# Attention, expert 0 and expert 1's first block ordered by a plan over the graph of steps

## The chip, the cores and the metric

The kernel runs on one core of one Trainium2 chip. The metric is the device time of one execution in microseconds (us). The engines are TensorE (PE: matmuls; PEld: its weight loads), VectorE (DVE), ScalarE (ACT), GpSimd (POOL) and SyncE (SP, which only issues DMAs). Each engine carries out its own instructions in the order in which the program gives them, and semaphores hold an instruction until what it reads or overwrites is ready.

## The reference

```python
def _attn_ref(q, k, v, mem_k, mem_v):        # (4, 8, 768, 64); 8 memory rows a head
    for c in range(768 // 32):               # chunks of 32 queries
        k_full = concat(mem_k, k[16 before .. 8 behind the chunk]); v_full likewise
        scores = q_c @ k_full.T / sqrt(64)
        a = exp(scores - max(scores)); a = a / (sum(a) + 1e-09)
        out[chunk] = a @ v_full

def _moe_ref(x, w_gate, w1, w2):             # x (3072, 512), 8 experts, 1024 hidden
    P = exp(x @ w_gate - max)
    for _ in range(8):
        P /= P.sum(1) + 1e-09; P /= P.sum(0) + 1e-09; P *= N / E
    return sum(P[:, e] * (relu(x @ w1[e]) @ w2[e]) for e in range(8))

def _moe2_ref(x, w_in, w_out):               # 512 -> 2048 -> 512
    h = relu(x @ w_in)
    return (h * h) @ w_out

reference = moe2(moe(attention(q, k, v, mem_k, mem_v)))
```

## The kernel before

Numbers are carried as pairs of 16-bit halves (hi and lo), so a product of two matrices is three matmuls: lo with hi, hi with lo, hi with hi.

Attention goes by 32 tiles of 96 queries (`NA`, `TQ`), each three chunks, against 120 keys and 8 memory rows. One tile is a chain of 22 steps: load q, k, v (`a_load`); the largest magnitude per row and over the tile (`a_scale`, `a_all`, `a_row_max`, `a_spread`, `a_scale2`); split into hi and lo (`a_split`, `a_split_lo`); transpose q and k by a DMA (`a_tqk`); scores with a mask (`a_scores`), their row maximum (`a_max`), its transpose (`a_mt`, `a_mtc`); the scores again, transposed, less the maximum (`a_st`); exponential (`a_exp`) and its split (`a_asplit`, `a_asplit_lo`); times v (`a_av`); normalization (`a_norm`), split (`a_xsplit`, `a_xsplit_lo`) and a DMA transpose into `xt` (`a_tx`), the input of the experts.

Expert 0 goes by 13 blocks of tokens (two of 128, then eleven of 256). A block's first layer is four pairs of 24 matmuls (`l1_pair`), each followed by a relu on ScalarE and its lo half on VectorE (`l1_lo`); the second layer has 24 matmuls for each 128 tokens, in two halves (`l2_half`). `gate` gives the logits of 128 tokens. When all logits are there, `balance_steps` runs the eight rounds of the reference's loop, with one column sum on PE in each. Expert 1's first block (`PLAIN`: 14 products `prod` and 8 second-layer halves) follows expert 0; its results wait in PSUM until the balance is done (`l2_acc`). From expert 1's second block on, loops of products with their own hooks order the rest of the kernel.

PSUM has eight banks. Two (`ps`) serve the experts and the gate; attention has one (`mm`) for the small transposes and maxima, three (`sc`) for scores and two (`av`) for the output. There are three load buffers for q, k and v (`raws`), two of them in memory that results need later, so `raw_of` uses three for 18 tiles and two after that. Where several steps share memory or a bank, the framework puts in the waits.

The order of this first stage is written out by time: every step has an offset within its tile (`STEPS`), every tile a start (`ta`: in the end 10.957 us after the last), the weights of expert 0 and 1, the gate and the balance have times of their own (`W_AT`, `TE`, `SK`), and expert 0's pairs and halves advance a clock of 2.65 us each, stretched by `STR`. The steps are sorted by these times and issued in that order:

```python
def when(i, n):
    r = min(1.0, i / RAMP)
    t = ta(i) + (1 - r) * STEPS[n][1] + r * STEPS[n][0]
...
ev.sort(key=lambda x: x[:2])
for _, _, fn, a in ev:
    fn(*a)
```

Lines of the profile: 265 the tile's maximum, 269 a cast behind it, 288 its spread, 343 and 485 the two DMA transposes, 361 mask and 373 scores, 408 and 411 transposed scores and what is subtracted, 441 to 449 the output, 458 to 461 normalization, 509 gate, 553 column sum, 594 weights of expert 0, 790 to 792 expert 0's first layer, 1285 to 1287 second layers, 929 products of expert 1 and later, 1299 adding expert 1's result.

## Time and profile before

| | us |
|---|---|
| median of three runs | 2578.11 |
| lowest, highest | 2573.98, 2579.66 |
| span of the profiled execution | 2577.2 |
| PE busy in it | 2426.7 (94%) |
| DVE, ACT, POOL busy | 1906.5, 1339.0, 1339.5 |
| start of expert 1's second block | 582.78 |

The profiled execution is one run of the program, and its span reaches from the first to the last instruction. PE's busy time counts overlapping matmuls once and is no measure of how close PE is to its best; the distance from one matmul's start to the next is. The granted clock is the share of PE's full speed (1.00 is 2.4 GHz, the lower level is 1.2 GHz, and a number between is a mean over the stretch). A time in brackets behind a timeline row is how long the engine stood idle before it, and what ended that.

### The profile page before, as it was taken

What the parts mean: (1) busy time and instruction counts of PE and PEld (TensorE: products, weight loads), DVE (VectorE), ACT (ScalarE), POOL (GpSimd) and SP (SyncE); (2) the same over time, 40 slices, a digit from 0 to 9 for tenths busy, and PEclk for the clock granted to TensorE, in tenths of its full rate; (3) what the DMA queues carried; (4) which work ended last, traced back from release to release, by engine and by line L of the source; (5) the groups of instructions that cost most, each with busy time, mean ns of one, the idle gap of its engine ahead of it and who ended that gap; (6) DMA issues with size and microseconds to landing.
All of it is one profiled execution on the core that took longest, in us unless ns stands there. A gap on an engine that the chain in (4) does not pass through costs nothing.

```text
span 2577.2 us, 53497 instructions
## 1 busy us (share of the span) xinstructions
PE 2426.7 (94%) x21970; PEld 2035.4 (79%) x21970; DVE 1906.5 (74%) x2932; ACT 1339.0 (52%) x2323; POOL 1339.5 (52%) x1120
## 2 busy tenths in 40 slices
PE   2789889889999999999999999999999989999999
PEld 1566566556668888888888888888888878888888
DVE  7778677476567888788788878877758887667555
ACT  4444444233344555556555555555556666766454
POOL 2312112352563675567557465746746767866443
PEclk9889899999999999999999999999999999999999
DMA  7688676232335345334444544443333366663221
GB/s 167 96 142 144 105 124 101 72 104 77 126 120 177 132 143 185 129 127 135 170 151 132 168 138 151 148 150 127 113 103 132 117 170 155 169 168 123 77 68 54
DMA packets 377916, 334.31 MB, mean 130 GB/s; under 512 B 256584, under 2 KB 311368, under 8 KB 371016
## 3 DMA queue, kind: packets, MB, share of 16 engines
q1 hardware_dynamic: 294054, 309.99, 41.8%
q10 hardware_dynamic: 83618, 20.91, 4.5%
q8 instruction: 171, 2.80, 0.4%
q14 instruction: 73, 0.60, 0.1%
HBM read 215.50 MB, written 77.07 MB: 114 GB/s over the span
## 4 chain that ended last, share of the span: by engine, by line
PE 79%; DVE 11%; DMA 3%; ACT 3%; issue 2%; POOL 2%; SPq 1%; ACTq 0%; DVEq 0%; POOLq 0%
PE pbA L929 35%; PE pbE L929 18%; PE pbB L929 8%; PE pb L929 4%; PE py L1285 3%; PE py L1286 3%; PE py L1287 3%; PE ph L790 1%; PE ph L792 1%; PE ph L791 1%; DVE amx L265 1%; DVE hp L1127 1%; DVE acc L1240 1%; DMA raw<-in_q_dram 1%; DMA qkT<-qk 1%
## 5 line engine op out<-in xcount | busy, mean ns | idle before, releaser
L929 PEld LDWEIGHTS <-wb 128*128 128x128 f16 x5184 | 508.3, 98 | 71.6 <-issue 10.4
L929 PEld LDWEIGHTS <-hp 128*128 128x128 f16 x4608 | 450.8, 98 | 57.9 <-DVE hp L1127 3.0
L929 PEld LDWEIGHTS <-wx 128*128 128x128 f16 x3888 | 380.8, 98 | 52.7 <-issue 7.6
L929 PEld LDWEIGHTS <-xt 128*128 128x128 f16 x3456 | 338.2, 98 | 48.4 <-DVE xt L1127 7.3
L929 PE MATMUL pbA<-w2p,hp 128*128 128x256 f16 x2304 | 291.4, 273 | 3.7 <-DVE hp L1127 1.9
L929 PE MATMUL pbA<-S,wb 128*128 128x256 f16 x2304 | 283.6, 273 | 6.5 <-ACT S L1057 2.7
L929 PE MATMUL pbE<-xt,wx 128*128 128x256 f16 x2304 | 284.1, 273 | 4.5 <-DVE u L1062 3.7
L1057 ACT ACTIVATE u<-pbA 128x512 f32<-128x512 f32 x180 | 106.5, 592 | 187.0 <-PE pbA L929 185.8
L432 POOL TENSOR_TENSOR aT<-e,aT 128x768 f16<-128x768 f32 x32 | 52.5, 1640 | 243.5 <-ACT aT L426 220.0
L929 PE MATMUL pbA<-w2p,xt 128*128 128x256 f16 x1152 | 157.1, 273 | 0.0
L929 PE MATMUL pbE<-xt,hp 128*128 128x256 f16 x1140 | 156.6, 274 | 0.0
L929 PE MATMUL pbE<-xt,xt 128*128 128x256 f16 x1140 | 156.2, 273 | 0.2 <-POOL xt L1127 0.2
L1285 PE MATMUL py<-w2p,hp 128*128 128x512 f16 x384 | 149.0, 388 | 7.0 <-DVE hp L799 3.7
L1057 ACT ACTIVATE xt<-pbA 128x512 f32<-128x512 f32 x147 | 86.5, 592 | 127.0 <-PE pbA L929 124.9
L1286 PE MATMUL py<-w2p,hp 128*128 128x512 f16 x384 | 149.0, 388 | 0.0
L1287 PE MATMUL py<-w2p,hp 128*128 128x512 f16 x384 | 148.7, 387 | 0.0
L1127 POOL TENSOR_TENSOR hp<-u,hp 128x512 f16<-128x512 f32 x86 | 114.8, 1335 | 64.9 <-ACT hp L1120 64.9
L929 PE MATMUL pbA<-S,wx 128*128 128x256 f16 x1152 | 141.4, 273 | 2.3 <-ACT xt L1057 0.9
L929 PE MATMUL pbB<-xt,wb 128*128 128x256 f16 x1152 | 141.4, 273 | 0.0
L929 PE MATMUL pbA<-xt,wb 128*128 128x256 f16 x1152 | 141.4, 273 | 0.0
L1062 DVE TENSOR_TENSOR u<-pbE,u 128x512 f32<-128x512 f32 x100 | 68.6, 686 | 94.8 <-ACT u L1057 54.9
L1127 POOL TENSOR_TENSOR xt<-u,xt 128x512 f16<-128x512 f32 x72 | 94.8, 1325 | 55.2 <-ACT xt L1120 55.2
(376 smaller groups left out, 5802.6 us busy)
## 6 DMA issues: line engine op xcount, KB each, us to landing
wst<-in_moe_w_dram SPq DMA_DIRECT2D x80, 512.0 KB
xt<-xdr SPq DMA_DIRECT2D x40, 1024.0 KB
S<-sdr SPq DMA_DIRECT2D x126, 256.0 KB
w2d<-wst SPq DMA_DIRECT2D x32, 512.0 KB
w2p<-w2d SPq DMA_DIRECT2D x32, 512.0 KB
wst<-in_moe_w_dram SPq DMA_DIRECT2D x56, 256.0 KB
...
```

Of the source, the lines that this page charges most:

```text
L265: nc.vector.tensor_reduce(mx, raw, AX.X, ALU.max, apply_absolute_value=True)
L432: nc.gpsimd.tensor_tensor(aT[:, 1], st.pop((i, "e")), aT[:, 0], ALU.subtract)
L790: nc.tensor.matmul(p[:, r], lhsT=w[:, 1], rhs=xh, start=first, stop=False)
L791: nc.tensor.matmul(p[:, r], lhsT=w[:, 0], rhs=xl, start=False, stop=False)
L792: nc.tensor.matmul(p[:, r], lhsT=w[:, 0], rhs=xh, start=False, stop=last)
L929: nc.tensor.matmul(p[:, r], lhsT=w[:, ws], rhs=x[:, xs], start=a, stop=z, skip_group_check=onto)
L1057: nc.scalar.activation(t, p, AF.Copy, scale=sc)
L1062: nc.vector.tensor_tensor(t, p, t, ALU.add)
L1127: eng.tensor_tensor(d[:, 1], t, d[:, 0], ALU.subtract)
L1285: nc.tensor.matmul(p, lhsT=h[:, 1], rhs=w[:, 0], start=first, stop=False)
L1286: nc.tensor.matmul(p, lhsT=h[:, 0], rhs=w[:, 1], start=False, stop=False)
L1287: nc.tensor.matmul(p, lhsT=h[:, 0], rhs=w[:, 0], start=False, stop=last)
```

## The change

The written times go. Every step of the stage, from the first load to the adding of expert 1's first block, becomes a task with an engine, a cost, a priority, the tasks that it comes after, and what it holds (PSUM banks, DMA semaphores). When the kernel is built, `Plan.run` takes again and again the task that can start first (among equals, the one of lowest priority number), and the steps are issued in the order of these starts. Attention's priorities are 100 a tile, expert 0's start at 10000.

With it come changes of the steps:

- `a_scores` and `a_st`: heads of 64 rows on either half of the array. hi x lo, lo x hi and hi x hi are three matmuls of 64 rows a head, where before one of 128 rows did two of them. The mask is 3 rows in place of 96, on rows 0 and 64 (`GRP`), and what `a_st` subtracts is 19 rows (`KR`) in place of 112. So q and k are 16 blocks to transpose, not 20, and GpSimd's copy of q's hi half is gone.
- `avb`: the small maxima and transposes and the gate's logits move into the second of the two banks of attention's output; scores get four banks.
- three load buffers for all tiles, two of them in memory of attention's own; tiles 0 and 2 are loaded by SyncE's queue, the others by ScalarE's; memory rows are loaded only when a buffer turns to another batch.
- `a_scale` and its followers read the upper halves of 32-bit numbers in place, which drops four small VectorE instructions a tile.
- the gate's scale goes through a matmul in place of a GpSimd reduction.
- first-layer pairs are cut in four pieces (`l1_mm`), second-layer halves in four (`l2_part`); weight splits, the balance's column sums and the sums for Strassen's products are cut likewise, so that each piece is one task on one engine.
- the mask set-up is rewritten (more small GpSimd instructions, and nine on ScalarE as three tasks).

The core of the diff:

```diff
+COST = {
+    "load": 1.3, "mx": 1.75, "row": 0.12, "row_mx": 0.28, "all": 0.12, "scale": 0.75, "invx": 0.25,
+    "hi": 1.85, "lo": 2.25, "tqk": 3.1, "scores": 0.95, "max": 1.65, "mt": 0.12, "mtc": 0.25,
+    "st": 1.0, "exp": 1.05, "ahi": 0.85, "alo": 1.7, "av": 0.8, "norm": 1.05, "xhi": 0.65,
+    "xlo": 0.7, "tx": 1.25,
 }
-TA = 10.957
...
-SK = [0.01, 2.7, 2.52, 7.55, 7.55, 7.27, 6.55, 7.55, 7.55, 7.89, 7.55, 7.55, 5.95]
-W_AT = [-5.06, 6.92, 9.11, 14.42, 18.96, 23.87, 33.67, 39.86, -3.33, 28.00, 3.81]
+LAND = {"load": 1.8, "tqk": 4.4, "tx": 1.7, "w": 2.5}
+SLACK = 0.6
+MOVE = {"load": 3.6, "tqk": 4.5, "tx": 1.5, "w1": 1.5, "w2": 1.3}
...
-    raws = [
-        ap_.tile([P, 3, H * D], F32, name="raw0"), acc[NB - 1][:, 0:3, :], acc[NB - 2][:, 0:3, :]
-    ]
+    raws = [ap_.tile([P, 3, H * D], F32, name=f"raw{n}") for n in range(2)]
+    raws.append(acc[NB - 1][:, 0:3, :])
...
-        return i % 3 if i < 3 * LATE // 4 else i % 2
-
+        return i % 3
+
+    avb = psa.tile([P, 2, 512], F32, name="avb")
+    mmb = avb[:, 1, 4 * VP:]
...
-        dq = nc.sync if i < 3 else nc.scalar
+        dq = nc.sync if i in (0, 2) else nc.scalar
...
-            dq.dma_start(
-                out=hd(raw[NW:P, t, :]), in_=mem[b].rearrange("h p d -> p h d")
-            )
+            if mem_in.get((raw_of(i), t)) != b:
+                mem_in[raw_of(i), t] = b
+                dq.dma_start(
+                    out=hd(raw[NW:P, t, :]), in_=mem[b].rearrange("h p d -> p h d")
+                )
...
-        eb = ap_.tile([P, 3], I32, tag="aeb0", name="aeb0", bufs=2)
-        e16 = ap_.tile([P, 3], BF16, tag="ae16", name="ae16", bufs=2)
-        nc.vector.tensor_scalar(eb, mx.bitcast(I32), EXP_MASK, None, ALU.bitwise_and)
-        nc.vector.tensor_copy(e16, eb.bitcast(F32))
-        st[i, "e16"] = e16
+        st[i, "amx"] = mx
 
     def a_all(i):
 
-        p = psa.tile([3, P], F32, tag="mm", name="pmax")
-        nc.tensor.matmul(p, lhsT=st.pop((i, "e16")), rhs=ident, start=True, stop=True)
+        p = mmb[0:3, 0:P]
...
-        scs = [psa.tile([TQ, 4, P], F32, tag="sc", name="sc", bufs=3) for u in range(2)]
-        for sc in scs:
+        scs = [psa.tile([TQ, 4, P], F32, tag="sc", name="sc", bufs=4) for u in range(2)]
+        for g, sc in zip(GRP, scs):
             nc.tensor.matmul(
                 sc,
-                lhsT=onehot,
-                rhs=maskr[:, mask_at(i)].unsqueeze(1).to_broadcast([TQ, 4, P]),
+                lhsT=onehot[g:g + NR],
+                rhs=less[g:g + NR, mask_at(i), 0].unsqueeze(1).to_broadcast([NR, 4, P]),
                 start=True,
                 stop=False,
             )
 
-        for s in range(2):
+        for s in range(3):
             for hh in range(4):
                 for u in range(2):
                     q_, k_ = qk_of(qkT, 2 * hh + u)[s]
                     nc.tensor.matmul(
-                        scs[u][:, hh, :], lhsT=q_, rhs=k_, start=False, stop=(s == 1 and hh == 3))
+                        scs[u][:, hh, :], lhsT=q_, rhs=k_, start=False, stop=(s == 2 and hh == 3))
...
-        p = psa.tile([TQ + 2 * H, TQ], F32, tag="mm", name="pmt")
-        nc.tensor.matmul(p, lhsT=m16s[i % 2], rhs=ident16, start=True, stop=True)
+        p = mmb[0:MR, P + 4:P + 4 + TQ]
...
-        for u in range(2):
-            for hh in range(4):
+        for hh in range(4):
+            for u, g in enumerate(GRP):
                 nc.tensor.matmul(
-                    scs[u][:, hh, :], lhsT=less[:, mask_at(i), 4 * u + hh], rhs=mt,
-                    start=False, stop=(hh == 3))
+                    scs[u][:, hh, :], lhsT=less[g:g + KR, mask_at(i), 4 * u + hh],
+                    rhs=mt[g:g + KR], start=False, stop=(hh == 3))
...
-        o = psa.tile([TQ, 2, 512], F32, tag="av", name="av")
+        o = avb[0:TQ]
...
-        lgp = ps.tile([P, 2, E], F32, tag="ps", name="lgp")
+        lgp = mmb[:, 228:228 + 2 * E].rearrange("p (s e) -> p s e", s=2)
...
-        def cols():
+        def cols_mm():
...
+            st["colsum"] = p
+
+        def cols():
+            p = st.pop("colsum")
...
+        return [load, start, rows] + [cols_mm, cols_rows] * (ITERS - 1) + [cols_mm, cols_end]
...
+    def l1_mm(fp, b, c, n, r, kks):
+
+        if r == 0 and kks[0] == 0:
+            st["l1", fp, b, c] = ps.tile([P, 2, n], F32, tag="ps", name="ph2")
+        p = st["l1", fp, b, c]
+        for kk in kks:
+            w = wb[kk % 2][fp % 2][:, :, 2 * (kk // 2) + fp // 2, r * P:(r + 1) * P]
+            xh, xl = xt[b][:, 0, kk, c:c + n], xt[b][:, 1, kk, c:c + n]
+            first, last = kk == 0, kk == KD - 1
+            nc.tensor.matmul(p[:, r], lhsT=w[:, 1], rhs=xh, start=first, stop=False)
+            nc.tensor.matmul(p[:, r], lhsT=w[:, 0], rhs=xl, start=False, stop=False)
+            nc.tensor.matmul(p[:, r], lhsT=w[:, 0], rhs=xh, start=False, stop=last)
+
...
+    def l2_part(e, t, tl, fs, ev):
+
+        if fs[0] == 0:
...
+        for f in fs:
...
+        class Plan:
+            LAG = {"PE": 0.25, "DVE": 0.1, "ACT": 0.1, "POOL": 0.1}
+
+            def __init__(self, rings):
+                self.tasks, self.bufs = [], rings
+                self.start, self.done = {}, {}
+
+            def add(self, eng, cost, pri, fn, *a, after=(), ring=None, land=0.0, lock=False, dma=0.0):
+                self.tasks.append([eng, cost, pri, fn, a, list(after), ring, land, lock, [], dma])
+                n = len(self.tasks) - 1
+                if ring and ring[0] == "lane":
+                    self.tasks[n][9] = [[n]] * ring[1]
+                return n
...
+            def run(self):
+                free, held, shut, moved = {}, {r: [] for r in self.bufs}, 0.0, 0.0
+                todo = {n: len(x[5]) for n, x in enumerate(self.tasks)}
+                users = {}
+                for n, x in enumerate(self.tasks):
+                    for d in x[5]:
+                        users.setdefault(d, []).append(n)
+                ready = {n: 0.0 for n, c in todo.items() if not c}
+                order = []
+                while ready:
+                    best = None
+                    for n, r in ready.items():
+                        eng, cost, pri, _, _, _, ring, _, lock, _, _ = self.tasks[n]
+                        t = max(r, free.get(eng, 0.0))
+                        if ring:
+                            name, m = ring
+                            for k_ in range(m):
+                                back = len(held[name]) + k_ - self.bufs[name]
+                                if back >= 0:
+                                    for f in self.tasks[held[name][back][0]][9][held[name][back][1]]:
+                                        t = max(t, self.seen(f, eng))
+                        if lock:
+                            t = max(t, shut)
+                        if t < 1e8 and (best is None or (t, pri, n) < best[0]):
+                            best = ((t, pri, n), n)
+                    assert best, [self.tasks[n][3:5] for n in ready]
+                    (t, _, _), n = best
+                    eng, cost, _, _, _, _, ring, land, lock, _, dma = self.tasks[n]
+                    self.start[n] = t
+                    self.done[n] = t + cost + land
+                    if dma:
+                        moved = max(moved, t + 0.5) + dma
+                        self.done[n] = max(self.done[n], moved + 1.8)
+                    if eng:
+                        free[eng] = t + cost
+                    if lock:
+                        shut = t + cost
+                    if ring:
+                        held[ring[0]].extend((n, k_) for k_ in range(ring[1]))
+                    order.append(n)
+                    del ready[n]
+                    for u in users.get(n, ()):
+                        todo[u] -= 1
+                        if not todo[u]:
+                            ready[u] = max(self.seen(d, self.tasks[u][0]) for d in self.tasks[u][5])
+                assert len(order) == len(self.tasks)
+                return [(self.start[n],) + tuple(self.tasks[n][3:5]) for n in order]
+
+        plan = Plan({"lane": 8, "lgp": 1, "pmax": 1, "pall": 1, "pmt": 1, "sc": 4, "av": 1, "ps": 2})
...
+        WAR = {
+            "load": [("lo", 3)], "mx": [("row", 2)], "row_mx": [("all", 2)],
+            "scale": [("lo", 2), ("invx", 2), ("exp", 6)], "hi": [("tqk", 2), ("av", NV)],
+            "tqk": [("st", 2)], "max": [("mt", 2)], "mtc": [("st", 2)],
+            "exp": [("alo", 1)], "ahi": [("av", 2)], "norm": [("xlo", 1)], "xhi": [("tx", 1)],
+        }
+        RING = {"row": ("pmax", 1), "all": ("pall", 1), "mt": ("pmt", 1), "scores": ("sc", 2),
+                "st": ("sc", 2), "av": ("av", 1), "tqk": ("lane", 1)}
+        FREE = {"row": ["row_mx"], "all": ["scale"], "mt": ["mtc"], "scores": ["max", "max"],
+                "st": ["exp", "exp"], "av": ["norm"]}
...
+        LS = [add("ACT", 3.2, 5 + 100 * mv, setup_less, mv) for mv in range(3)]
         for i in range(NA):
...
+            for r, (n, fn) in enumerate(FN.items()):
+                pri = 100 * i - r - (300 if n == "load" else 0)
+                cost = COST[n]
+                eng = ENG[n]
+                if n == "load" and i in (0, 2):
+                    eng = "SP"
+                    cost = 2.5
+                ring = RING.get(n)
+                if n == "load":
+                    ring = ("lane", 3 + 2 * (i % TPB in (0, TPB - 1)) + 2 * (i % TPB < 3))
+                if n in ("tx", "invx"):
+                    two = i * TQ % (P if n == "invx" else BLK) // 32 + 3 > (4 if n == "invx" else 16)
+                    cost *= 2 if two else 1
+                    ring = ("lane", 1 + two) if n == "tx" else None
+                after = [T[i, d] for d in RAW.get(n, ())]
+                after += [T[i - m, d] for d, m in WAR.get(n, ()) if i >= m]
+                after += [T[i - 1, n]] if i and n not in MOVE else []
+                after += LS[mask_at(i):mask_at(i) + 1] if n == "scores" else []
+                T[i, n] = add(eng, cost, pri, fn, i, after=after, ring=ring,
+                              land=LAND.get(n, 0.0), dma=MOVE.get(n, 0.0), lock=n in ("lo", "xlo", "alo", "invx"))
...
+        for w in range(2):
+            pri = (150, 350)[w]
+            for n in range(4):
+                m = 4 * w + n
+                W["load", m] = add("SP", (0.9, 0.5)[w], (-150, 60)[w], (w1_load0, w2_load0)[w], n,
+                                   after=[] if w == 0 else [T[1, "tqk"]], land=LAND["w"],
+                                   dma=MOVE["w1"], ring=("lane", 2 - w))
+                W["max", m] = add("DVE", 1.22, pri, w_max0, m, after=[W["load", m]])
...
+            for f in range(NF // 2):
+                w_in_ = [W["lo", n] for n in range(4)]
+                war = [L2[x] for x in L2 if blk > 1 and x[0] == blk - 2]
+                part = None
+                for r in range(2):
+                    for kks in ((0, 1), (2, 3)):
+                        part_ = add("PE", 0.655 * f_, pri + f, l1_mm, f, b, c, n0, r, kks,
+                                    after=[part] if part else x_in + w_in_, ring=None if part else ("ps", 1))
+                        m0, part = (m0 if part else part_), part_
+                m1 = part
+                rl = add("ACT", 0.15 + 0.45 * f_, -4, l1_relu, f, b, c, n0, blk % 2, after=[m1] + war)
+                lo = add("DVE", 0.15 + 0.55 * f_, -4, l1_lo, f, b, c, after=[rl])
+                holds(m0, lo)
...
+        OP = add("SP", 1.5, -9, open_post, after=list(T.values()) + list(G.values()), land=LAND["w"])
...
+        prev, accs = L2[len(blocks) - 1, 1, 1], {}
+        for n, (item, hooks) in enumerate(zip(PLAIN, jobs(1, 0))):
+            u = item[2] if item[1] == "P" else 1
+            need = [x for c_ in WC[2 * u:2 * u + 2] for x in c_]
+            if item[1] == "L2":
+                need = W2C[2 * item[3]:2 * item[3] + 2]
...
         ev.sort(key=lambda x: x[:2])
         for _, _, fn, a in ev:
+            fn(*a)
+        for _, fn, a in plan.run():
             fn(*a)
```

## Rows read from the trace of the kernel before

**Rows 1.** Windows: busy us of PE, PEld, DVE, ACT, POOL; clock, DMA share, GB/s

```profile
0.00:86.00 86.00, 25.37 (x233) 18.89 (x234) 65.97 (x169) 37.51 (x54) 23.00 (x30) 0.90 0.76 151
...
150.00:275.00 125.00, 116.97 (x1275) 85.24 (x1272) 102.42 (x236) 58.73 (x119) 25.92 (x38) 1.00 0.83 134
275.00:325.00 50.00, 39.94 (x374) 27.16 (x374) 32.23 (x82) 17.96 (x36) 7.60 (x11) 0.86 0.66 101
325.00:478.00 153.00, 142.78 (x1551) 104.42 (x1550) 101.67 (x239) 66.03 (x133) 28.73 (x37) 1.00 0.60 98
478.00:582.80 104.80, 85.58 (x517) 52.48 (x515) 71.92 (x132) 35.49 (x51) 51.01 (x44) 0.92 0.33 113
582.80:2577.20 1994.40, 1966.58 (x17462) 1708.85 (x17461) 1485.89 (x1971) 1094.04 (x1872) 1185.33 (x939) 1.00 0.42 133
```

**Rows 2.** Timeline, 0 to 16 us: start, us, engine or queue, line, instruction

```profile
0.72 5.24 SPq L594 DMA_DIRECT2D acc<-in_moe_w_dram  x8
...
15.76 1.75 DVE L265 TENSOR_REDUCE amx<-raw 128x3 f32<-128x1536 f32 x1 [6.65 <-DMA raw<-in_q_dram]
```

**Rows 3.** Timeline of PE: first products of expert 0 and expert 1's block 1

```profile
86.04 0.30 PE L790 MATMUL ph<-xt,wb 128*128 128x128 f16 x1
...
582.78 0.60 PE L929 MATMUL pb<-xt,wb 128*128 128x256 f16 x4 [2.29 <-DVE acc L1299]
```

**Rows 4.** Groups on PE, 150 to 275 us: busy us, mean ns, idle before

```profile
L790 PE MATMUL ph<-xt,wb 128*128 128x256 f16 x120 | 32.8, 273 | 0.3 <-ACT lg L509 0.3
...
L1285 PE MATMUL py<-w2p,hp 128*128 128x512 f16 x56 | 21.3, 380 | 0.0
```

**Rows 5.** Timeline of PE at 480 us, second layer of expert 0

```profile
480.72 0.38 PE L1285 MATMUL py<-w2p,hp 128*128 128x512 f16 x1
...
481.15 0.38 PE L1287 MATMUL py<-w2p,hp 128*128 128x512 f16 x1
```

**Rows 6.** Timeline of PE, 187 to 193 us: transposed scores, then scores

```profile
187.81 0.78 PE L408 MATMUL sct<-qkT 128*128 128x96 f16 x16
188.52 0.51 PE L411 MATMUL sct<-mt,less 112*128 112x96 f16 x8
188.96 0.16 PE L288 MATMUL pall<-ad,ones 128*128 128x3 bf16 x1
...
191.60 0.60 PE L361 MATMUL sc<-less,onehot 96*96 96x512 bf16 x2
192.04 0.61 PE L373 MATMUL sc<-qkT 128*96 128x128 f16 x8
...
192.58 0.42 PE L373 MATMUL sc<-qkT 64*96 64x128 f16 x8
...
192.93 0.28 PE L790 MATMUL ph<-xt,wb 128*128 128x256 f16 x1
```

**Rows 7.** DMA queues, 150 to 275 us: packets, MB, share of engines

```profile
q1 hardware_dynamic: 34816, 10.10, 54.3%
q10 hardware_dynamic: 25948, 6.49, 28.1%
```

**Rows 8.** Groups on VectorE, 150 to 275 us: a small one

```profile
L269 DVE CAST ae<-aeb 128x3 bf16<-128x3 f32 x10 | 1.7, 172 | 0.3
```

**Rows 9.** Timeline of VectorE at 200 us: normalization of one tile

```profile
200.38 0.15 DVE L458 TENSOR_SCALAR rs<-av 96x8 f32<-96x8 f32 x1
...
200.80 0.69 DVE L461 TENSOR_TENSOR acc<-av,rs 96x512 f32<-96x512 f32 x1
```

**Rows 10.** Timeline of SyncE's queue at 477 us: the last tile's transpose

```profile
477.62 1.21 SPq L485 DMA_TRANSPOSE xt<-x  x1
```

**Rows 11.** Timeline of PE, 527 to 578 us: column sums, expert 1's product

```profile
527.95 0.49 PE L553 MATMUL colsum<-pm,ones 128*128 128x192 f32 x2
528.28 0.93 PE L929 MATMUL pb<-xt,wb 128*128 128x256 f16 x7
...
577.41 0.49 PE L553 MATMUL colsum<-pm,ones 128*128 128x192 f32 x2
```

553 lines of the change are left out of this document (267 added, 286 removed).

## The prediction

> **What bounds the kernel now.** I read the page first (its slices show where TensorE, PE, is not full), then the busy time by stage, and inside one steady stretch the groups of instructions, the timeline of one tile's attention and the DMA queues. The plan orders only what runs before expert 1's second block, and that block's first product starts at 582.78 us [rows 3]. What follows, 1994.4 us with PE busy for 1966.6, is the same text in both kernels [rows 1]; I carry it over unchanged. So the question is when that product starts.
>
> In the first 582.8 us PE is bound in part only. From 150 to 275 us it is busy for 117.0 of 125 us at full clock, and from 325 to 478 for 142.8 of 153 [rows 1]: there it is the bound. Elsewhere it is starved: 25 of the first 86 us, and 39.9 of 50, at a granted clock of 0.86, from 275 to 325 [rows 1]. The first product of expert 0 starts at 86.04 us [rows 3]. From 478 on, when the last tile of attention is transposed (issue at 477.62 [rows 10]), PE is busy for 85.6 of 104.8 us at a clock of 0.92 [rows 1], while the balance chain goes on to its last column sum at 577.41 [rows 11].
>
> What PE has to do there, at steady rates: 256-column matmuls follow each other at 0.11 us (four span 0.60 [rows 3], one takes 0.27 [rows 4]), 512-column ones at 0.215 (480.72 to 481.15 for two [rows 5]). Expert 0's first layer is 13 blocks, two of half width, of 4 x 24 matmuls: 1152 full ones, 126.7 us. Its second layer is 24 x 24 x 0.215 = 123.8. Expert 1's first block is 168 x 0.11 + 96 x 0.215 = 39.1. Eight column sums at 0.33 (527.95 to 528.28 [rows 11]) are 2.6. For attention I take what is left of the steady stretch: 3 x 120 x 0.11 + 3 x 56 x 0.215 = 75.7 us are expert 0's [rows 4], so 49.3 of 125 us went to ten tiles (the count of [rows 8]), 4.9 each with gates, changes of shape and short waits; 32 tiles make 157. Sum 449. The stage took 582.8, so 134 us are PE waiting or slowed.
>
> **The change, part by part.** *Rows of 64.* One tile's scores run from 191.60 to 192.93, 1.33 us; the transposed scores from 187.81 to 188.96, 1.15 [rows 6]. Eight 128-row matmuls span 0.61 us, eight 64-row ones only 0.42, so with the last one's 0.22 taken off they follow at 0.056 and 0.03: two of 64 rows on different halves run side by side [rows 6]. After: 24 of 64 rows at 0.03 are 0.72, the two mask matmuls (now 3 rows, one on either half) 0.22 in place of 0.44, a change of shape 0.09 (192.43 to 192.58, less one pitch): 1.03. The transposed scores: 24 at 0.025 (96 columns) and 8 at 0.0275 are 0.82. Saved: 0.63 a tile; I take 0.6, 19 us in all. Bounds: nothing, if matmuls of 3 and 19 rows do not pair or change the shape too often, and 0.75.
>
> The Trainium skill, "TensorEngine Tiling (Array Packing)", section Key Properties, says that a change of tiling mode drains TensorE, and lists tiles of 32 rows as a mode of their own. By that rule 3 and 19 rows would be another mode than 64, two more changes a tile; at 0.09 each that is 6 us and the sum would give 2500 in place of 2494. No trace here has a matmul of so few rows.
>
> *Less work beside PE.* The transpose of q and k has 16 blocks in place of 20, with x's eight 24 in place of 28: queue q1's 54.3% of 125 us for ten tiles is 6.8 a tile [rows 7] and falls to 5.8; the loads (q10, 28.1%, 3.5 a tile) lose most of the memory rows, about 0.1. Together 9.2 a tile. VectorE (DVE) had 102.4 us for ten tiles [rows 1], 10.2 each; four small instructions go (such as the cast at 0.17 [rows 8]), about 0.75: 9.5. GpSimd loses a copy, ScalarE a quarter of its split instructions. The gate's scale leaves GpSimd's reduction for one matmul and some small DVE instructions, once. None of these ends the path while PE is full, so I cost them at nothing; their cover is PE's own 250.5 / 32 + 4.3 = 12.1 us a tile. They matter as the pace that attention can reach when it goes first: 9.5.
>
> *The start.* Before, SyncE's queue issues eight weight loads (0.72 to 5.96) ahead of tile 0's loads, and DVE's first maximum starts at 15.76 [rows 2]. Now tile 0 goes first: about 8 us. Against that, ScalarE's nine mask instructions stand ahead of tile 1's load on its queue and wait for some twenty small GpSimd instructions. Up to the first product DVE was busy for 66 of 86 us [rows 1], which is over six tiles' worth, where two tiles and four weight maxima are needed: the plan takes the earlier tile first. I put the first product at 60, about midway between 35 (two tiles' DVE time after the first load) and the old 86. About three tiles' attention, 13 us of PE, lies in front of it, so 47 us are lost. Second-layer weights are loaded after tile 1, and a 256-token block needs 2.7 tiles: 8 us more for feeding (0 to 25).
>
> *Small pieces, plan, tail.* Attention has priority, and first-layer pairs (2.6 us) are cut in four. Attention can then end near 50 + 31 x 10.2 = 366 us, with expert 0 far from done. From 478 the first product of expert 1 (528.28) is 50 us off and the balance's last sum 99 [rows 11]; from 370 both are over by 470, under PE's leftover work. What is late next is PE itself, so the 19 us of idle PE there go, and the starved stretch at 275 goes as well, since tiles now have three load buffers throughout. Four score banks end a wait that I count within the 4.9.
>
> *One shared bank.* The added wait: maxima, their spread, the row-maximum transpose, the gate and half of attention's output now lie in one PSUM bank. If the program guards the bank as a whole, each of these five matmul groups waits for the reader of the one before, and behind it on PE's queue stand expert 0's pieces. The readers hold it about 2.1 us of a 10-us tile (the normalization 1.1, from 200.38 to the end of the row at 200.80 [rows 9]; I take 0.25 for each of the others), so a fifth of 4.75 writes meets one, for some 0.45 us: 14 us over 32 tiles. Bounds: 0 and, with every second write held for a whole split (1.8 us), 3.6 a tile.
>
> **Sum.** 250.5 + 39.1 + 2.6 + 32 x 4.3 = 429.8; start 47, feeding 8, bank 14: block 1 starts at 498.8 in place of 582.8, 84 us earlier. The profiled execution's 2577.2 becomes 2493.2; the median of the runs is 0.9 above it: 2494.
>
> **Rivals.** With a fixed order the end is also first tile + 31 x pace + what the plan left for after attention. At a planned 9.5 us a tile PE gets 5.2 us of expert 0 beside each, 161 in all, and 89 + 41.7 = 131 stay behind. So 50 + 31p + 131: a pace of 10.25 gives my 499.
>
> (a) *Transfers set the pace.* DMA was 83% busy in the steady stretch [rows 1], and its need of 9.2 us a tile is nearly the planned pace; a transpose landing late holds the scores, and everything queued behind them on PE. At 11.5: 537.5, 2533 us. Against: the bytes fall, and before, the queues held 12.5 us a tile with PE full. 0.17.
>
> (b) *The shared bank, slower than before.* From a pace of 13 on, 2.7 us a tile over mine, the end is past 582.8. That takes two waits a tile of 1.4 us on readers queued behind DVE's longer instructions, with DVE 82% busy [rows 1] and to be fuller. At a pace of 14: 615, 2610 us. The Trainium skill, "PSUM — Partial Sum Buffer", section PSUM bank collisions raise a hardware error, speaks for it: no two engines may touch one bank on the same partitions at once, so waits have to guard the bank and not the address. No run here shows such sharing. Against: most readers take under 0.3 us. 0.13.
>
> (c) *The start does not move*: weights, mask set-up and first tiles still meet at 86. 429.8 + 86 - 18 + 22 = 520, 2515 us. 0.13.
>
> (d) *PE full from 50 on*, no bank or feeding loss, and attention at 4.0: 420 + 37 = 457, 2452 us. 0.12.
>
> **How the numbers follow.** My case, 2465 to 2530: 0.40. No difference (a measurement of this kernel tells 0.2% at best, 5 us; that is (a) at a pace near 13): 0.05. Faster: 0.40 + 0.17 + 0.13 + 0.12 = 0.82; slower 0.13. A range of 2450 to 2575 leaves out (b) and a little more.
>
> **What would show it.** Right: expert 0's first product near 60; the eight-and-eight patterns of scores at 1.0 us and transposed scores at 0.8; no dip at 275 to 325; attention's last transpose near 370 while expert 0 goes on past 450; a product of expert 1's second block near 500; the same 1994 us after it. Wrong: gaps on PE ahead of attention's output or the maxima, released by DVE's normalization (b); gaps ahead of scores released by the transpose (a); a first product at 80 or later (c); another length of the later part.

## The result, and the profile after

The changed kernel takes 2531.24 us (median; 2530.39 to 2532.41) where the kernel before takes 2577.52: a ratio of 0.9818, 95% interval 0.9804 to 0.9832. That is 46 us less; the forecast was 84 less (2494), inside the range but short by nearly half. The first question is in which stage the difference lies. Busy time by stage of the changed kernel's profiled execution (span 2529.5; columns as in [rows 1]: the stretch, its length, busy time of PE, PEld, DVE, ACT and POOL with counts, granted clock, DMA share, GB/s; the DMA share adds up the times of the packets that start in the stretch, so that a short one can come out above 1):

```profile
0.00:87.50 87.50, 26.89 (x353) 20.27 (x354) 66.88 (x139) 46.96 (x60) 31.46 (x51) 1.00 0.77 147
87.50:150.00 62.50, 50.08 (x685) 38.29 (x686) 41.94 (x87) 26.83 (x55) 8.21 (x14) 0.92 0.85 128
98.00:105.00 7.00, 0.57 (x11) 0.47 (x9) 1.32 (x2) 0.00 (x0) 0.14 (x1) 0.92 1.33 145
150.00:275.00 125.00, 117.67 (x1535) 81.62 (x1535) 104.38 (x223) 62.90 (x117) 25.90 (x33) 1.00 0.94 140
275.00:325.00 50.00, 49.54 (x617) 34.91 (x617) 35.29 (x76) 24.11 (x48) 9.11 (x11) 1.00 0.81 126
325.00:422.00 97.00, 94.48 (x1191) 66.52 (x1184) 60.02 (x129) 44.12 (x87) 15.62 (x17) 1.00 0.51 78
422.00:535.30 113.30, 101.97 (x656) 64.95 (x654) 75.14 (x135) 38.70 (x57) 50.27 (x44) 0.94 0.31 104
535.30:2529.50 1994.20, 1966.54 (x17463) 1708.99 (x17461) 1487.46 (x1971) 1093.96 (x1872) 1186.72 (x939) 1.00 0.42 133
```

The last row is the part after expert 1's second block has begun: 1994.2 us, 1994.4 before. The whole gain is the 47.5 us by which that block starts earlier, and the dip at 275 to 325 of [rows 1] is gone. 28.0 of them are time in which TensorE was idle (122.7 us before the second block, now 94.7). Where the stage begins and ends, on TensorE's timeline (start, duration, line, output and inputs; in brackets the wait before it) and, last, on SyncE's for the end of attention:

```profile
87.38 0.31 PE L361 MATMUL avb<-ident,m 96*83 96x96 f16 x1 [4.67 <-DVE m L355]
87.48 0.31 PE L784 MATMUL ph<-xt,wb 128*128 128x128 f16 x1
...
535.26 0.93 PE L930 MATMUL pb<-xt,wb 128*128 128x256 f16 x7
...
421.77 1.21 SPq L455 DMA_TRANSPOSE xt<-x  x1
```

Expert 0's first product is at 87.48: it has not moved (86.04 in [rows 3]; forecast 60). The second block starts at 535.26 instead of 582.78. Attention's last transpose is issued at 421.77 instead of 477.62 [rows 10]. The forecast had both earlier, near 499 and 366.

One tile's matmuls in the steady stretch, to set beside [rows 6] (scores, then transposed scores):

```profile
196.60 0.41 PE L329 MATMUL sc<-less,onehot 3*96 3x512 bf16 x2
196.95 0.87 PE L341 MATMUL sc<-qkT 64*96 64x128 f16 x24
197.75 0.39 PE L1291 MATMUL py<-w2p,hp 128*128 128x512 f16 x1
...
202.00 0.68 PE L378 MATMUL sct<-qkT 64*128 64x96 f16 x24
202.62 0.34 PE L381 MATMUL sct<-mt,less 19*128 19x96 f16 x8
```

From the first start to the last end, scores take 1.22 us and transposed scores 0.96; in [rows 6] the same is 1.40 and 1.22. From the first start to the start of the next instruction, which is how the prediction read [rows 6], scores take 1.15 instead of 1.33 (196.60 to 197.75) and transposed scores mostly 0.89 instead of 1.15 in those rows (mostly 1.07 in that trace).

### The profile page after: what moved, and what is told of

It reads as the page before. It is cut to its first block, busy times and chain, and to the rows that moved or that the text cites. A ratio compares the mean times of both kernels' runs of the same rounds, so it can differ in the third digit from the quotient of the medians.

```text
span 2529.5 us, 54257 instructions
## 1 busy us (share of the span) xinstructions
PE 2407.2 (95%) x22483; PEld 2015.5 (80%) x22483; DVE 1871.1 (74%) x2759; ACT 1337.6 (53%) x2294; POOL 1327.3 (52%) x1108
## 4 chain that ended last, share of the span: by engine, by line
PE 82%; DVE 12%; ACT 2%; DMA 2%; issue 1%; POOL 1%; ACTq 0%; SPq 0%; DVEq 0%; POOLq 0%
PE pbA L930 36%; PE pbE L930 18%; PE pbB L930 8%; PE pb L930 4%; PE py L1291 3%; PE py L1292 3%; PE py L1293 3%; PE ph L784 1%; PE ph L786 1%; PE ph L785 1%; DVE hp L1128 1%; DVE acc L1241 1%; PE sc L341 1%; DVE smx L350 1%; PE sct L378 1%
## 5 line engine op out<-in xcount | busy, mean ns | idle before, releaser
L1291 PE MATMUL py<-w2p,hp 128*128 128x512 f16 x384 | 147.6, 384 | 7.6 <-DVE hp L921 6.0
L1292 PE MATMUL py<-w2p,hp 128*128 128x512 f16 x384 | 147.1, 383 | 0.0
L1293 PE MATMUL py<-w2p,hp 128*128 128x512 f16 x384 | 146.9, 383 | 0.0
```

Source lines behind the costliest of these rows:

```text
L1291: nc.tensor.matmul(p, lhsT=h[:, 1], rhs=w[:, 0], start=first, stop=False)
L1292: nc.tensor.matmul(p, lhsT=h[:, 0], rhs=w[:, 1], start=False, stop=False)
L1293: nc.tensor.matmul(p, lhsT=h[:, 0], rhs=w[:, 0], start=False, stop=last)
```

## The experiments

All are edits of the changed kernel. Their times stand in one table, with the points of the trace that turned out to matter: expert 0's first product, the issue of the transpose of tile 6 (counted from 0, as everywhere here) and of the last tile, and the first product of expert 1's second block, in us.

| kernel | median | ratio to before, 95% | first product | tile 6 | last tile | second block |
|---|---|---|---|---|---|---|
| the changed kernel | 2531.2 | 0.9804 to 0.9832 | 87.5 | 145.2 | 421.8 | 535.3 |
| mask | 2529.8 | 0.9800 to 0.9838 | 85.4 | 139.9 | 420.3 | 534.8 |
| xbuf | 2550.2 | 0.9874 to 0.9915 | 80.2 | 144.0 | 438.1 | 555.2 |
| sc3 | 2549.8 | 0.9864 to 0.9909 | 87.1 | 145.8 | 431.7 | 555.9 |
| bank | 2533.2 | 0.9812 to 0.9849 | 86.9 | 139.2 | 413.6 | 537.0 |
| bank2 | 2533.5 | 0.9807 to 0.9839 | 87.5 | 142.6 | 422.0 | 536.8 |
| w2dve | 2529.4 | 0.9786 to 0.9823 | 87.2 | 142.7 | 419.8 | 530.4 |
| pieces | 2542.7 | 0.9843 to 0.9874 | 88.1 | 143.3 | 431.4 | 546.4 |
| recost | 2538.0 | 0.9824 to 0.9860 | 80.3 | 141.3 | 415.9 | 540.0 |
| spload | 2519.0 | 0.9751 to 0.9784 | 83.7 | 136.4 | 410.0 | 524.0 |
| nolo | 2529.1 | 0.9788 to 0.9818 | 82.7 | 139.0 | 416.7 | 530.4 |
| now2 | 2533.8 | 0.9806 to 0.9836 | 87.9 | 145.7 | 423.8 | 539.9 |
| three | 2514.2 | 0.9739 to 0.9766 | 83.6 | 134.1 | 407.4 | 518.1 |

The kernel before was run again beside each group of these kernels, and its median lay between 2577.5 and 2580.2: differences of under 3 us between two rows of the table are not told apart.

Read the last two columns first: the second block starts 111 to 124 us after the last tile, whatever was edited. Now read the column of the first product against the median: it says nothing. The two earliest, 80.2 and 80.3, belong to kernels slower than the changed one.

### The start: mask set-up, or the order of the queues?

In the trace of the changed kernel ScalarE's queue begins with the nine mask instructions. They wait for GpSimd, tile 1's load goes out only between them (12.38 to 15.16), and tile 0's split (line 300) comes after them all, though VectorE has its scale ready at 11.5:

```profile
6.52 1.05 ACT L1462 ACTIVATE less<-heads 83x1024 bf16<-83x1024 bf16 x1 [2.38 <-POOL heads L1432]
9.13 2.13 ACT L1465 ACTIVATE less<-maskr 3x1024 bf16<-3x1024 bf16 x2 [1.55 <-POOL maskr L1459]
...
12.38 0.63 ACTq L217 DMA_DIRECT2D raw<-in_k_dram  x1
...
18.77 1.33 ACT L300 ACTIVATE qk<-raw,asc 128x512 f16<-128x512 f32 x2
```

**mask** moves them and nothing else:

```diff
+        order = plan.run()
+        masks = [x for x in order if x[1] is setup_less]
+        order = [x for x in order if x[1] is not setup_less]
+        for x, i in zip(masks, (0, 1, 2)):
+            order.insert(1 + [y[1:] for y in order].index((a_split, (i,))), x)
```

> The changed kernel with its order kept, except that the nine mask instructions (three calls of setup_less) go to ScalarE's queue behind the splits of tiles 0, 1 and 2, instead of ahead of tile 1's load. Theory M (the mask set-up at the head of ScalarE's queue is why the start did not move): tile 0's split, at 18.8 us in the changed kernel, comes at about 12, tile 1's maximum several us before its 19.4, the first product of expert 0 at about 80 instead of 87.5, and the median falls from 2531 to about 2524. Theory Q (what holds the first product is the order of the queues behind it: tile 1's output is normalized at 60.7 but its split waits until 73.6 and its transpose until 81.2 behind work of later tiles): the first tiles come earlier, the first product stays within 2 us of 87.5, and the median within 3 us of 2531.

Tile 1's load went out at 0.79 and tile 0's split ran at 15.32 (not 12: VectorE's first maximum now starts at 11.29 instead of 7.63, behind tile 0's load, which shares the transfers with tile 1's). The first product came at 85.4, not at 80, and the time is the same within the measurement. Theory M falls.

Further down the queue the order is the obstacle. Tile 1's output is normalized from 60.66 on (the row of line 428 on VectorE's timeline). On ScalarE's timeline its split (line 440) then stands behind tile 2's steps and the conversion of second-layer weights:

```profile
65.46 0.25 ACT L367 ACTIVATE mt<-avb 83x96 f16<-83x96 f32 x1 [8.64 <-PE avb L361]
...
71.43 1.13 ACT L652 ACTIVATE acc<-acc,w1sc 128x1024 f32<-128x1024 f32 x1
72.59 1.06 ACT L655 ACTIVATE w2p<-acc 128x1024 f16<-128x1024 f32 x1
73.56 0.61 ACT L440 ACTIVATE x<-acc 96x512 f16<-96x512 f32 x1
```

The plan itself had put it there, since x16 has one buffer and tile 0's transpose must be over. **xbuf** gives tiles 0 to 16 a second one:

```diff
+        if i % 2 == 0 or i > 15:
             x = ap_.tile([TQ, 2, 2, 4, D], F16, tag="x16", name="x16")
+        else:
+            x = acc[NB - 2][0:TQ, 0, :].bitcast(F16).rearrange(...)
...
+                back = 2 if i < 17 else 1
+                after += [T[i - back, "tx"]] if n == "xhi" and i >= back else []
```

> The changed kernel with two buffers instead of one for the split of x (x16) in tiles 0 to 16; the plan is told. In the plan's own times tile 1's split then follows its normalization at once (53.8 instead of 66.0), and the first product comes at 67.4 instead of 74.8; the rest of the order stays nearly as it was. Theory Q (the order that the plan wrote is what held tile 1's end back): on the chip tile 1's transpose comes some 7 to 15 us before 81.2, the first product at 73 to 80 instead of 87.5, and the median falls by 5 to 12 us, to 2519 to 2526. Theory M (set-up and first tiles): the first product stays at 85 or later, the median within 3 us of 2531.

The mechanism is as theory Q has it, and the consequence is not. On SyncE's timeline of xbuf tile 1's transpose is issued at 64.38 instead of 81.18:

```profile
64.38 1.21 SPq L458 DMA_TRANSPOSE xt<-acc  x1
...
92.03 2.12 SPq L458 DMA_TRANSPOSE xt<-x  x1
```

The first product came 7.3 us earlier, but tile 2's transpose later (92.03; 89.12 in the changed kernel), tile 6's only 1.2 earlier and the last tile's 16.3 later: the new plan leaves a hole of 37 us between two tiles' scores, from 220 to 257. 19 us slower. Both theories were about the first product; neither tells the time.

**nolo** and **now2** take work away that I had put beside the first tiles at no cost.

```diff
     def w_lo0(n, d):
-        nc.gpsimd.tensor_tensor(flat(d[:, 1]), flat(stage0[n]), flat(d[:, 0]), ALU.subtract)
+        pass
```

> The changed kernel in its own order, with GpSimd's eight subtractions for the low halves of expert 0's weights left out (about 2.1 us each in 34 to 87 us; the halves are zero from fills at the start, so this part of the computation is left out). Beside them small VectorE instructions last about 2 us instead of 0.2 (lines 191, 194 and 355). Theory W (the preparation of expert 0's weights, which I had put beside the first tiles at no cost, is what holds the tiles back): the first product comes at 80 or earlier, lost time of TensorE up to 150 us falls by 6 us or more from its 85, the median is 2519 to 2526. If the queues' order and the transfers set the start: first product at 85 to 88, the median within 3 us of 2531.

```diff
     def w2_load0(n):
-        nc.sync.dma_start(out=stage0[4 + n], in_=w2_ap[0, n])
+        pass
```

> The changed kernel in its own order, with the four loads of expert 0's second-layer weights (512 KB each, issued at 32 to 33.7 us) left out; VectorE fills the tiles in place of their maxima, so that its time stays about the same. What is left out: that layer's weights are a constant. Theory D (in the start the transfers stand in each other's way: DMA is busy for 0.82 of the first 75 us, and transposes of q and k take 9 us and more to land): tiles 2 to 5 come 5 us or more earlier, the first product at 80 to 84, the median 2518 to 2526. If the transfers of the weights are hidden: first product at 86 to 88, the median within 3 us of 2531.

Of nolo, the small VectorE instructions of the first 87.5 us (groups: busy time, mean ns), first in the changed kernel, then in nolo:

```profile
L355 DVE TENSOR_TENSOR m<-smx,m 96x16 f16<-96x16 f32 x5 | 4.8, 950 | 0.2
L194 DVE TENSOR_SCALAR asc<-ainv 128x3 int32<-128x3 int32 x7 | 4.5, 637 | 0.2
L191 DVE TENSOR_SCALAR ainv<-aeb 128x3 int32<-128x3 int32 x7 | 3.6, 513 | 0.6
```

```profile
L191 DVE TENSOR_SCALAR ainv<-aeb 128x3 int32<-128x3 int32 x7 | 1.3, 182 | 0.6
L194 DVE TENSOR_SCALAR asc<-ainv 128x3 int32<-128x3 int32 x7 | 1.2, 175 | 0.2
...
L355 DVE TENSOR_TENSOR m<-smx,m 96x16 f16<-96x16 f32 x5 | 0.9, 178 | 0.2
```

GpSimd's subtractions did stretch them to three to five times their length; without them the first product comes 4.8 us earlier, and the median is 2 us lower, which this measurement hardly tells from nothing (the profiled execution, 2526.2, is the fastest of its four). The transfers of the second layer's weights were hidden (now2). No single suspect explains the start at 87.

### The plan's durations

**recost** gives the plan the durations that the trace shows.

```diff
-    "hi": 1.85, "lo": 2.25, "tqk": 3.1, "scores": 0.95, "max": 1.65, "mt": 0.12, "mtc": 0.25,
-    "st": 1.0, "exp": 1.05, "ahi": 0.85, "alo": 1.7, "av": 0.8, "norm": 1.05, "xhi": 0.65,
+    "hi": 1.85, "lo": 2.25, "tqk": 4.5, "scores": 1.15, "max": 1.65, "mt": 0.12, "mtc": 0.25,
+    "st": 1.05, "exp": 1.05, "ahi": 0.85, "alo": 1.9, "av": 1.15, "norm": 1.05, "xhi": 0.65,
...
+        S0 = add("POOL", 9.0, -999, lambda: None)
```

> The changed kernel with the plan's durations set to what its own trace shows: scores 1.15 (0.95), transposed scores 1.05, attention output 1.15 (0.8), GpSimd's subtraction 1.9 (1.7), issue of the transpose of q and k 4.5 (3.1) and its landing 5.0, and the mask set-up not before 9.0 us. Nothing else changes but the order that follows. Theory P (the order is made for shorter durations than the chip's, and the queues, which keep it, stall where the plan was too early): the lost time of TensorE before expert 1's second block falls by 10 us or more, 2510 to 2522. If the order's errors in time don't matter, or a greedy plan is as good or bad by accident: 2525 to 2550.

7 us slower, on the edge of what the intervals tell apart, and far from theory P's gain, although its first product came at 80.3. TensorE is idle for 94.7 us before the second block, as in the changed kernel; the granted clock is lower, 0.83 from the first product to 150 us (0.92 in the changed kernel) and 0.93 instead of 1.00 from 150 to 275. Better durations alone did not make a better order: the plan takes whatever can start first, and a change of input gives another order.

### The shared bank and the fourth score bank

**sc3** takes the fourth score bank away, **bank** gives the bank so freed to the small results; both have the same order.

```diff
-        scs = [psa.tile([TQ, 4, P], F32, tag="sc", name="sc", bufs=4) for u in range(2)]
+        scs = [psa.tile([TQ, 4, P], F32, tag="sc", name="sc", bufs=3) for u in range(2)]
```

```diff
-    mmb = avb[:, 1, 4 * VP:]
+    mmb = psa.tile([P, 512], F32, name="mmb")
```

> The changed kernel with three score banks instead of four, the plan told; the shared bank stays. It undoes the part of the four banks and is what the next run is compared with. If the fourth bank is worth something: TensorE's 8 score and transposed-score groups wait for the readers of the pair before, about 0.5 us a tile, 10 to 16 us in all, 2541 to 2547. If TensorE's leftover work fills such waits anyway: within 4 us of 2531.

> As the run with three score banks, in the same order, but with the bank that this frees given to the small results (the maxima, their spread, the row maxima, the gate), so that attention's output has its two banks alone. Theory B (the shared bank costs what I forecast, 14 us, as waits on TensorE behind other readers): 10 us or more less than the run with three score banks, and the waits of the attention output and of the row maxima behind other tiles' readers go. If the sharing is nearly free: within 3 us of the run with three score banks.

The difference of the two is 16.6 us, and their intervals don't meet: with three score banks the sharing costs about what I had forecast (14). TensorE's three longest waits from 87.5 us to the second block, by line and releaser (us, times, longest), of sc3 and then of bank:

```profile
PE avb L361 <- DVE acc L431: 8.3, 8, 2.8
PE py L1291 <- DVE hp L921: 7.3, 1, 7.3
PE avb L411 <- ACT lg L482: 7.0, 2, 6.7
```

```profile
PE py L1291 <- DVE hp L921: 7.4, 1, 7.4
PE avb L419 <- POOL aT L402: 3.6, 3, 1.5
PE avb L411 <- ACT aT L396: 3.5, 2, 3.4
```

Two entries go: the row maxima's transpose behind another tile's normalization (8.3) and an attention output behind the gate's copy (7.0), both waits for a neighbour in the bank and not for data. 6.7 of the 7.0 are a single wait, which the next section explains by something else than the bank. sc3 is 18.6 us slower than the changed kernel, more than either theory said, but not by waits for a score bank: in all of sc3's stretch TensorE waits 1.0 us for one (line 329). sc3 has an order of its own, and xbuf shows that a new order alone can cost 19 us; what the fourth bank is worth by itself stays open. Three banks with the small results apart (2533) and four with them shared (2531) are equal.

**bank2** keeps four score banks and the changed kernel's order, and makes two tiles of the shared one.

```diff
-    avb = psa.tile([P, 2, 512], F32, name="avb")
-    mmb = avb[:, 1, 4 * VP:]
+    avs = [psa.tile([P, 512], F32, name=f"avb{g}") for g in range(2)]
+    mxb, mmb = (t[:, 4 * VP:] for t in avs)
```

> The changed kernel in exactly its own order, with four score banks, but the shared two-bank tile is two tiles of a bank each: heads 0 to 3 with the tile maxima and their spread in one, heads 4 to 7 with the row maxima and the gate in the other; the normalization takes two instructions more a tile. A wait on a reader then holds one bank's writers, not both. Theory B (sharing costs TensorE about 16 us, the difference of the two runs with three score banks): half of the pairs of writer and reader go, 4 to 12 us less, 2519 to 2527; the 6.9 us wait of an attention output behind the gate's copy in 87 to 150 us shrinks or moves. If the sharing costs little once there are four score banks: 2529 to 2533, or up to 3 us more for the added VectorE instructions.

No gain; theory B's 4 to 12 us are not there. The gate still shares a bank with half of the output, and the largest wait stays (from 87 to 150 us):

```profile
PE avb L411 <- ACT lg L483: 6.4, 1, 6.4
```

### Why that copy was late: loads in a compute engine's queue

The copy itself takes 0.18 us. In the changed kernel from 98 to 105 us every engine all but stands still (the third row of the first table: TensorE 0.57, VectorE 1.32, ScalarE 0) while the transfers' share is the highest of the table. ScalarE's timeline, then the chain of waits:

```profile
104.86 0.32 ACTq L236 DMA_DIRECT2D acc<-in_q_dram  x1
105.23 0.18 ACT L482 ACTIVATE lg<-avb 128x16 f32<-128x16 f32 x1 [8.36 <-DMA acc<-in_v_dram]
```

```profile
95.22 9.62 DMA qkT<-qk
...
104.86 0.32 ACTq L236
...
105.23 0.19 ACT lg L482
...
105.47 0.21 PE avb L411
```

Tile 8's load of q (the text below calls it tile 7's; it is the ninth) waits for the transpose of q and k that was issued eight transfers earlier (the kernel uses eight lanes in turn) and lands after 9.62 us. The load's issue stands in ScalarE's queue, so the gate's copy waits for it, the attention output waits for the copy's bank, and expert 0's pieces wait behind the output. **spload** issues all loads from SyncE's queue, in the same order:

```diff
-        dq = nc.sync if i in (0, 2) else nc.scalar
+        dq = nc.sync
```

> The changed kernel in its own order, with the loads of all tiles issued from SyncE's queue instead of ScalarE's (tiles 0 and 2 already were). In the changed kernel ScalarE's queue stands still from 97.9 to 104.9 us behind the issue of tile 7's load of q, which waits for the transpose of q and k issued at 95.22 to land (9.62 us); the gate's copy stands behind it, an attention output waits 6.9 us for that copy's bank, and in 98 to 105 us TensorE is busy for 0.57, VectorE for 1.32, ScalarE for 0. Theory L (load issues in ScalarE's queue hold the engine, and TensorE through it): the stall at 98 goes, lost time of TensorE in 87 to 150 us falls by 6 to 10, and some 2 to 3 us waits later go: 2515 to 2525. Against it: the loads now stand behind SyncE's transposes, which wait for VectorE's low halves; then tiles come later, and the time is 2535 or more.

spload, columns as in the first table:

```profile
87.50:150.00 62.50, 56.98 (x796) 43.11 (x790) 51.42 (x106) 28.96 (x59) 10.54 (x13) 0.95 0.88 148
150.00:275.00 125.00, 119.42 (x1531) 82.13 (x1531) 101.60 (x222) 64.01 (x121) 25.72 (x35) 0.99 0.78 135
```

In 87.5 to 150 TensorE is busy for 57.0 us instead of 50.1; tile 6's transpose comes 8.8 us earlier, the last tile's 11.8, and the median falls by 12.2. Theory L holds. TensorE is idle 3.7 us less before the first product, 6.9 less from there to 150 us and 1.7 less from 150 to 275. The load itself waits less, too: it goes out 6.0 us after that transpose (97.43 and 91.43). The 3.7 are another matter than the stall at 98: tile 1's load no longer stands among the mask instructions either. The Trainium skill, "Perfetto Trace Analysis", section DMA Optimizations, says that balancing DMAs across the engines that can issue them may help if the issuing itself is the bottleneck. No row here shows that condition; the reverse paid, because an issue that waits holds the compute instructions behind it.

### Small pieces

**pieces** undoes the cut of expert 0's steps:

```diff
-                for r in range(2):
-                    for kks in ((0, 1), (2, 3)):
-                        part_ = add("PE", 0.655 * f_, pri + f, l1_mm, f, b, c, n0, r, kks, ...)
+                m0 = part = add("PE", 2.62 * f_, pri + f, l1_all, f, b, c, n0, after=x_in + w_in_, ring=("ps", 1))
```

> The changed kernel with its small pieces undone: a first-layer pair of expert 0 is one task of 2.6 us instead of four, a second-layer half one task instead of four; the plan is made anew. If the cut is what lets attention keep its pace: attention's last transpose comes 10 to 20 us later than 421.8 and the median is 10 us or more above 2531. If TensorE is full either way and the cut only adds changes between shapes: within 5 us of 2531, on either side.

11.5 us slower, with the last tile 9.6 us later, as the first theory has it: the cut lets attention keep its pace. The order is a new one here too, so that not all of the 11.5 need be the cut's.

### The tail

After 422 us attention is over and TensorE has only expert 0's rest and expert 1's first block. Its waits there, in the changed kernel:

```profile
PE py L1291 <- DVE hp L921: 6.0, 2, 3.9
PE ph L784 <- DVE hp L796: 3.8, 1, 3.8
PE py L1291 <- DVE wma L630: 1.5, 1, 1.5
```

For the first of them, rows of VectorE's and GpSimd's timelines and then of TensorE's (others lie between):

```profile
495.15 0.69 DVE L921 SCALAR_TENSOR_TENSOR hp<-u,hp 128x512 f16<-128x512 f32 x1
497.33 2.14 POOL L730 TENSOR_TENSOR w2p<-wst,w2p 128x1024 f16<-128x1024 f32 x1 [4.24 <-ACT w2p L727]
497.80 2.22 DVE L921 SCALAR_TENSOR_TENSOR hp<-u,hp 128x512 f16<-128x512 f32 x1
503.82 2.31 POOL L730 TENSOR_TENSOR w2p<-wst,w2p 128x1024 f16<-128x1024 f32 x1 [1.72 <-ACT w2p L727]
504.07 2.62 DVE L921 SCALAR_TENSOR_TENSOR hp<-u,hp 128x512 f16<-128x512 f32 x1
...
511.79 0.61 PE L1291 MATMUL py<-w2p,hp 128*128 128x512 f16 x1 [3.95 <-DVE hp L921]
```

The same VectorE instruction takes 0.69 us alone and 2.2 to 2.6 beside a GpSimd subtraction. The Trainium skill, "SBUF — State Buffer", section SBUF: two separate sides, calls the port pair of the two engines an exclusive lock, held for a whole instruction; these rows agree (497.80 to 500.02 reaches 0.55 past the end of GpSimd's instruction at 499.47). **w2dve** moves the four subtractions to VectorE:

```diff
     def w2_lo(e, i):
-        nc.gpsimd.tensor_tensor(
+        (nc.vector if e == 1 else nc.gpsimd).tensor_tensor(
```

> The changed kernel with one part of the tail moved: the four subtractions that give the low halves of expert 1's second-layer weights (2.13 to 2.31 us each on GpSimd, from 490.9 to 506.1) go to VectorE. Three of VectorE's instructions on line 921 last 2.1 to 2.6 us beside them, the others of the same shape 0.68, and TensorE waits 3.9 and 2.1 us for two of line 921 after 507, then runs at half clock until 520. Theory T (the two engines get in each other's way there, and that is the tail's loss): all of line 921 at 0.7, the two waits gone, 5 to 10 us less, 2521 to 2526. Against it: VectorE gets 4 times about 1.2 us more in a stretch where it is busy for 9.8 of 10 us; then the waits stay and the time is within 3 us of 2531.

Line 921's median falls from 0.90 to 0.68 us and the waits behind it from 6.0 to 4.0: the one of 3.95 shrinks to 0.68, the other grows from 2.08 to 3.35, behind three additions of line 939 that stand before line 921 in VectorE's queue in both kernels. The profiled execution's second block is 4.9 us earlier (it is the fastest of its four runs), the median 1.8 lower, with intervals that overlap. Theory T is right about the rows; its gain of 5 to 10 us is not shown.

**three** puts spload, mask and w2dve together, one diff after the other as shown.

> Three edits together, in the changed kernel's own order: all tile loads from SyncE's queue, the mask set-up behind the first splits, and expert 1's four weight subtractions on VectorE. Alone they gave 2519.0, 2529.8 and 2529.4 us where the changed kernel has 2531.2. If each removes a wait of its own, the gains add: 12.2 + 1.4 + 1.8 = 15.4, 2516 us. If the loads on SyncE's queue had already taken tile 1's load from behind the mask set-up, the mask's part is in it twice and the sum is 2517 to 2519; the tail's part is apart from both, and TensorE's waits behind line 921 after 500 us should fall from 6.0 to about 4 us.

2514.2: 17.1 under the changed kernel and 64 under the one before (ratio 0.9752). That is the sum of 15.4 within the measurement. The largest part and the tail's add up; whether the mask set-up adds anything is not shown, since the first product comes at 83.6 and came at 83.7 in spload. It is the fastest of all kernels here.

## Why the prediction was right in sign and short in size

In the prediction's own accounting, with the counts of the trace of after. Until 87.5 us four tiles of attention stand against 87.5 us. From 87.5 to 422 the need is 1035 first-layer matmuls, 192 of them of half width (939 x 0.11), 432 of the second layer (x 0.215) and 28 tiles; from 422 to 535.3 it is 212 x 0.11, 240 x 0.215, 168 x 0.11 and eight column sums at 0.33. What is left over in a stretch is its loss.

| step | forecast, us | measured, us |
|---|---|---|
| part after the second block's start | 1994.4 | 1994.2 |
| attention on TensorE, a tile | 4.3 | 4.6 |
| start | 47 | 69.1 (87.5 less 4 x 4.6) |
| feeding and shared bank, 87.5 to 422 | 22 | 9.5 |
| tail, from 422 | 0 | 17.3 |
| start of the second block | 498.8 | 535.3 |

**Right.** Only the stage before the second block changed; the dip at 275 went; from 150 to 422 us, where PE was to be full, the other engines cost little (10 us of idle TensorE in 272). The forecast's 498.8 + 32 x 0.3 + 22.1 + 17.3 - 12.5 is 535.3. No run undoes the rows of 64, or keeps the written times with the new steps, so these shares are read from the traces and not from runs that differ in one part.

**Rows of 64** was mis-sized. 4.6 is found as the 4.9 was: 125 us less 336 x 0.11 and 169 x 0.215 is 51.7, over 11.3 tiles (12 groups of scores, 12 of transposed scores, 10 of outputs). That saves 0.3 a tile, not 0.6; like the 4.9 it holds the short waits of its stretch (7.3 us of idle time after, 8.0 before). Rows of single tiles give 0.36 to 0.44 (1.33 and 1.07 to 1.15, now 1.15 and 0.89). Either way the term was too large, and the error can be seen in the prediction: 1.33 and 1.15 run to the start of the next instruction and hold the change of shape at the group's end, 1.03 and 0.82 were sums of pitches without it; 1.15 and 0.89 were measured. The rule of the Trainium skill on tiling modes, "TensorEngine Tiling (Array Packing)", Key Properties, which would have made 2500, is not borne out for the 19-row matmuls: 24 transposed scores at 0.025 are 0.60, and the first 19-row matmul starts 0.62 after the first of them.

**The start** is the step that failed most, by 22 us, and rival (c) was right on its sign: the first product at 87.5. The 60 was a point half way between two bounds, and the ground for it, "the plan takes the earlier tile first", is wrong. The plan takes what can start first and asks the priority only among equals. The forecast counted two tiles and four weight maxima on VectorE; in the first 87.5 us VectorE found the maxima of seven tiles and all eight weight maxima:

```profile
L590 DVE TENSOR_REDUCE wmx<-acc 128x1 f32<-128x1024 f32 x8 | 9.4, 1204 | 0.0
L247 DVE TENSOR_REDUCE amx<-raw 128x3 f32<-128x1536 f32 x5 | 8.7, 1747 | 10.9 <-DMA raw<-in_q_dram 10.9
...
L247 DVE TENSOR_REDUCE amx<-acc 128x3 f32<-128x1536 f32 x2 | 3.5, 1750 | 0.0
```

The chain followed back from the program's end runs on VectorE for 50.8 of the first 87.4 us, and the first product stands in TensorE's queue behind the row maxima of tile 4, for which TensorE waited 4.67 us (87.38). Taking single things away moved little: mask, nolo and now2 moved the first product by 2, 5 and 0 us and the median by 1.4, 2.1 and -2.6. xbuf and recost moved it by 7 us and got slower. So the step was also wrong in kind: an earlier first product alone does not make an earlier end. No run gave the first two tiles precedence on VectorE; what that would gain stays open. The start was slow, too: the first five groups of scores span 2.10 to 2.13 us instead of 1.22, although the view gives a clock of 1.00 there.

**The pace, and what it leaves.** In the prediction's own formula 50 + 31p + 131 the measured values are 60.2 (tile 0's transpose), 11.66 (421.8 less 60.2, by 31) and 113.5; the forecast had p = 10.25, which is 44 us of it. The 131 should not have been fixed: at a slower pace TensorE does more beside attention, and 17.5 us less were left. So the pace alone does not tell the end either: bank and recost have their last tile 8.2 and 5.9 us before the changed kernel's and take 2.0 and 6.8 us more. What does add up is TensorE's time before the second block: idle time, time lost to a granted clock under 1.00 while it was busy, and a rest of 428 to 433 us in all fourteen traces. Idle and lost time are 122.7 and 27.8 us before, 94.7 and 9.2 in the changed kernel, 81.7 and 10.1 in spload, 80.5 and 7.6 in three, 94.7 and 16.0 in recost, 101.8 and 17.0 in pieces, 103.0 and 23.7 in xbuf, 103.9 and 19.3 in sc3.

Rival (a)'s 11.5 a tile and its 2533 us are what came out, though not by its mechanism. On the chain from the first product to the last tile's transpose, transfers take 13.0 of 334 us, 9.62 of them the one transpose above; in the kernel before they take 55.9 of 392. None of TensorE's waits from 87.5 us to the second block is for a transfer. And at nearly the same pace from tile 6 on (10.9 a tile; 11.1 in the changed kernel), spload has a DMA share of 0.78 in 150 to 275 where the changed kernel has 0.94. Transfers hold attention at one place, through the load in ScalarE's queue, for 7 us; they do not set its pace.

**The tail** was costed at nothing with PE as cover ("what is late next is PE itself"). PE was not cover enough: 11.3 us are waits behind VectorE, and the other 6 fit the lower clock after them (0.94 on average from 422 on, and the lower level, 0.50, from 511.8 to 520, right behind the 3.95 us wait).

**The shared bank** came out near its size (14; 16.6 between bank and sc3), in part by luck: the sum was of many waits of 0.45 us, and one wait of 6.7 us behind the gate's copy, held by a load, is a large part of the 16.6. In the changed kernel TensorE's waits on the shared tile behind another step's reader add up to about 20 us, 6.9 of them that one. That the waits in sc3's rows are for the bank is as the Trainium skill has it ("PSUM — Partial Sum Buffer", section PSUM bank collisions raise a hardware error). **Four score banks**, "a wait that I count within the 4.9": sc3 is 18.6 us slower, but hardly by that wait (1.0 us), so the price of the fourth bank is not known.
